# Attention and experts in float32: in each first product one of seven inner products moved to the end, onto a sum that ScalarE puts into PSUM

## The chip, the cores and the metric

The kernel runs on one core of a Trainium2 chip. The metric is the device time of one execution in microseconds (us); the time before is the median of three runs. One further execution was taken by the profiler, and all readings of instructions come from that one. TensorE is called PE in the profile, VectorE DVE, ScalarE ACT, GpSimd POOL, and SyncE, which issues most transfers, SP.

## The reference

All arrays are float32. A block-wise linear attention with decay is followed by four dense experts whose outputs are added with weights.

```
# attention: B,H,S,D = 4,8,768,64; blocks of 64 positions
intra = (qb @ kb.T) * Dmask            # Dmask[i,j] = lam^(i-j) for i >= j
out_b = intra @ vb + (qb * lam^(i+1)) @ state
state = lam^64 * state + (kb * lam^(63-i)).T @ vb
x = out -> (B*S, H*D) = (3072, 512)

# experts: N,D,E,F = 3072,512,4,1024
p = domain_probs / (domain_probs.sum(-1) + 1e-9)
out = sum over e of p[:, e] * (relu(x @ w1[e]) @ w2[e])
```

## The kernel before

**Tiles.** The 3072 tokens are three groups of 1024. A *unit* is one group with one expert, twelve in all (`units`). For a unit the *first product* is relu(x @ w1), the *second product* is that times w2. TensorE works on the second product of one unit and the first product of the next unit in turn.

**The recursion.** Each first product is done with seven products instead of eight (Strassen's scheme in Winograd's form), and each of these seven again with seven. The outer seven are run in the order `SEQ`: M1, M5, M6, M2, M7, M3, M4. Each outer product is what the texts call a *group*: seven inner products, one step of `inner(i)` each, in the order `INNER`. An inner product is two matmuls (two records each in the trace) of 128x128 weights by 128x256 tokens. It writes a PSUM bank of 128x512 (`pg`). The scheme adds inner products up: M1, M6, M5 and M3 all add into the bank `g1`, and M7 and M4 into the bank `g3`; M2 takes `g3` anew. After each inner product the bank is read out (`READ`), since the partial sum is itself a summand of one of the four blocks ("quarters") of the result: after M1 block 11, after M7 block 22, after M6 block 21, after M4 it is added to 21, after M5 to 22, after M2 to 11, after M3 block 12. ScalarE copies (L1055) where nothing older is to be added, otherwise VectorE adds (L117, through the helper `tt`).

Three of the outer products, M2, M3 and M4 (`OUT`), finish a quarter of the unit's result. ScalarE then applies Relu in SBUF (L1059). In units 5 to 11 (`NEST` is 5), whose second product is also done with two levels of seven, GpSimd then multiplies the quarter by the tokens' gates (`gated`, queued in `aside`).

**The order of TensorE's work.** It is written out by hand in *slots*, eight to each outer product. With a are the steps of the first product, with b those of the second, each list being handed out two by two or one by one:

```
order = [b[0:2], a[0:2], b[2:4], a[2:4], b[4:6], a[4:6], b[6:8], a[6:8]]    # both nested
order = [b[0:1], a[0:2], b[1:2], a[2:4], b[2:3], a[4:6], b[3:5], a[6:8]]    # second product not nested
```

So a[4:6], the fifth and the sixth inner product, stand directly one after the other, and a piece of the second product stands before and after the pair. Between slots, planned work of VectorE and GpSimd is taken from the lists `background`, `lately`, `own_sums` and `aside`, and a planner (`pump`) starts transfers and weight sums by estimated times of the engines. The engines then execute their own instructions in the order in which they were written.

**Attention** of the second and third group runs in the same slots: `turn` (transposes), `scores` (L694, L701) four slots later, `values` ten slots later. The attention's tokens that come through DRAM (`comes_across`) have other distances. The first group's attention and the first product of the first unit (`direct_product`, tiles `pM` and `pc`, L1502) run ahead of all slots.

**Gates.** `gates` computes p on VectorE during the direct product and then lays it out with 32 small VectorE copies (L571, L573): 16 into `gate`, 16 into `last_gate`.

Of the kernel before, what the change touches and what calls it, by code (L numbers as in the profile page):

```python
# [11 lines left out]
AF = mybir.ActivationFunctionType  # L12
ALU = mybir.AluOpType
# [8 lines left out]
def kernel(  # L22
# [30 lines left out]
    nc = tc.nc  # L53

    B, H, S, D = q.shape
    E, DM, F = moe_w1.shape
    NTOK, DOUT = out.shape
    P = nc.NUM_PARTITIONS
# [3 lines left out]
    NCH = S // C  # L62
    CPG = 8
    G = CPG * C
    NG = NTOK // G
    Q = G // 4
    DH = DOUT // 2
    W = 512
# [20 lines left out]
    def bank(tag, name):  # L89
        return ps.tile([P, W], FP32, name=name, tag=tag)  # L90
# [25 lines left out]
    def tt(eng, o, a, b, op):  # L116
        eng.tensor_tensor(out=o, in0=a, in1=b, op=op)  # L117
        if eng is nc.gpsimd:
            busy[0] = max(busy[0], now[0]) + math.prod(o.shape[1:]) / (640 if spare else 480)
        else:  # L120
            vector(math.prod(o.shape[1:]), PSUM in (a.space, b.space))

    def vector(n, psum):
        filled[0] = max(filled[0], now[0] + psum / 2) + 0.09 + n * (0.31 if psum else 0.8 if spare else 0.49) / 512
# [11 lines left out]
    LAST = NG - 1  # L136
    ORDER = {0: (0, 1, 2, 3), 1: (1, 2, 3, 0), LAST: (2, 3, 0, 1)}
    units = [(g, e) for g in range(NG) for e in ORDER[g]]
    unit_of = {u: x for x, u in enumerate(units)}
    NEST = 2 * E - 3  # L140
    FINAL = len(units) - 1

    def token(g, half, x):
        c, b = (half, x) if g == 0 else (2 * g + x % 2, 2 * (x // 2) + half)
        return b * S + c * C

    def where_of(n):
        return n // CPG, n % CPG // 4, n % 4
# [173 lines left out]
    INNER = ("M1", "M7", "M6", "M4", "M5", "M2", "M3")  # L322
# [145 lines left out]
    def comes_across(n):  # L468
        return where(n)[0] >= SECOND
# [47 lines left out]
    for r in range(2):  # L517
        for ac in range(NHP):
            h = 4 * r + ac
# [31 lines left out]
    gates_of = decay[:, 7, 0:96].rearrange("p (t e) -> p t e", e=E)  # L551
# [7 lines left out]
    def gates():  # L559
        total = decay[:, 6, 96:120]  # L560
        nc.vector.reduce_sum(out=total, in_=probs, axis=AX.X)
        nc.vector.tensor_scalar_add(out=total, in0=total, scalar1=1e-9)
        nc.vector.reciprocal(out=total, in_=total)
        nc.vector.tensor_tensor(
            out=gates_of, in0=probs, in1=total.unsqueeze(2).to_broadcast([P, NTOK // P, E]), op=ALU.mult,
        )

        for n in range(NG * CPG):
            t = token(*where_of(n)) // P
            if n < LAST * CPG:  # L570
                nc.vector.tensor_copy(out=gate[:, n], in_=gates_of[:, t])  # L571
            if n >= CPG:
                nc.vector.tensor_copy(out=last_gate[:, (n - CPG) * E:(n - CPG + 1) * E], in_=gates_of[:, t])  # L573

    def turn_gates():
        p, o = bank("s0", "gp"), small("gr")
# [101 lines left out]
    def scores(n, tags):  # L678
        all_added()
        while n not in turned:  # L680
            take(lately, True)
        qT, kT = turned[n][0:2]
        while any(f in lately for f in turned[n][3:]):
            take(lately, True)
        begin_state(n)
        kd, vn = nat.pop((n, "kd")), nat[n, "v"]
        first, last = where(n)[0] == 0, where(n)[0] == NCH - 1

        sp = [bank(tags[r], "sp") for r in range(2)]
        blk = [slice(x * BL, (x + 1) * BL) for x in range(2)]  # L690
        for ac in range(NHP):
            for r in range(2):
                for x in range(2):
                    nc.tensor.matmul(  # L694
                        out=sp[r][half[x], ac * BL:(ac + 1) * BL], lhsT=hc(kT)[half[r], ac, blk[x]],
                        rhs=hc(qT)[half[r], ac, blk[x]], start=(ac == 0), stop=True, skip_group_check=True,
                    )
        for ac in range(NHP):
            for x in range(1 if last else 2):
                for r in range(2):  # L700
                    nc.tensor.matmul(  # L701
                        out=sp[x][half[r], 256 + ac * D:256 + (ac + 1) * D], lhsT=kd[half[x], 2 * ac + r],
                        rhs=vn[half[x], 4 * r + ac], start=False, stop=True, skip_group_check=True,
                    )
        st = small("st")
        added = [sp[x][:, 256:512].rearrange("p (h d) -> p h d", d=D) for x in range(2)]

        def mask(r):
            tt(
                nc.vector, st[:, r * 256:(r + 1) * 256], sp[r][:, 0:256], s_decay[:, r].rearrange("p h c -> p (h c)"),  # L710
                ALU.mult,
            )

        def middle():
            s = states[n][:, 1]
            if first:
                nc.scalar.copy(out=s, in_=added[0])
            else:
                tt(nc.vector, s, s, added[0], ALU.add)

        def end():
            s = states[after_of(n)] = small("kv")[:].rearrange("p (x h d) -> p x h d", x=2, d=D)
            passed(nc.vector, s[:, 0], states[n][:, 1])
            tt(nc.vector, s[:, 0], s[:, 0], added[1], ALU.add)

        work = [lambda: (mask(0), mask(1)), middle] + ([] if last else [end])
        soon(n, *work)
        masked[n] = st, work
# [86 lines left out]
    def attention(g):  # L815

        def put(slot, f):
            steps.append((slot, f))

        for i in range(CPG):  # L820
            n, s = g * CPG + i, BEGIN[g][0] + BEGIN[g][1] * i
            put(s - 10, lambda n=n: load_more(n))
            put(s - 6, lambda n=n: load(n, "v"))
            put(s, lambda n=n: turn(n, ("s0", "s1")))
            if comes_across(n):
                put(s - 2, lambda n=n: (decayed(n), nat.pop((n, "k"))))
            put(s + (6 if comes_across(n) else 4), lambda n=n: scores(n, ("s0", "s1")))
            put(s + (12 if comes_across(n) else 10), lambda n=n: values(n, ("s0", "s1")))
            if n == NG * CPG - 1:
                put(s + 17, turn_gates)  # L830
        steps.sort(key=lambda s: s[0])
# [40 lines left out]
    outer = {e: {n: {} for n in ("B11", "B12", "B21", "B22", "T1", "T2", "T3", "T4")} for e in range(NEST, len(units))}  # L872
    within = {}

    def gated(e, i, j, at, t):

        def step():
            n = j * 4 + (int(at[1]) - 1) * 2
            x = t[:].rearrange("p (c t) -> p c t", c=2)
            by = gate_bc[:, n:n + 2].rearrange("p n t -> p (n t)").unsqueeze(1).to_broadcast([P, 2, 256])  # L880
            tt(nc.gpsimd, x, x, by, ALU.mult)
            outer[e][f"B{i + 1}{j + 1}"][at] = t

        aside.append(after(2, step))
# [133 lines left out]
    def settle(m, blocks):  # L1018

        while m in ("M7", "M4") and blocks["left"]:  # L1020
            rest(force=True)

    def first_product(g, e, m, blocks, tags):

        while (g, e, m) not in fed:
            pump(force=True)
        while unit_of[g, e] in (1, 2 * E) and to_do.get(m):
            take(own_sums, True)
        until(("x", g, m))
        ws, t = fed.pop((g, e, m)), slots[m]  # L1030
        xs = {i: t[:, X_AT[i]] for i in X_AT}
        settle(m, blocks)
        old = {
            "M1": None, "M5": None, "M6": blocks.get("M1"), "M2": blocks.get("M1"), "M7": blocks.get("U2"),
            "M3": blocks.get("U4"), "M4": blocks.get("U3"),
        }[m]
        new = {n: small("m" + n) for n in ("11", "12", "21", "22")} if m in ("M1", "M5", "M6") else old
        banks = {}

        def inner(i):  # L1040
            t = tags[0] if i in ("M1", "M6", "M5", "M3") else tags[1]
            fresh = i in ("M1", "M7", "M2")
            if fresh:
                banks[t] = bank(t, "p" + t)
            p = banks[t]
            for j in range(2):
                nc.tensor.matmul(  # L1047
                    out=p[:, j * 256:(j + 1) * 256], lhsT=ws[i][:, j * P:(j + 1) * P], rhs=xs[i],
                    start=(fresh and j == 0), stop=True, skip_group_check=True,
                )  # L1050
            at, begins = READ[i]
            if not begins:
                tt(nc.vector, new[at][:], p[:], new[at][:], ALU.add)
            elif old is None:
                nc.scalar.copy(out=new[at][:], in_=p[:])  # L1055
            else:
                tt(nc.vector, new[at][:], p[:], old[at][:], ALU.add)
            if m in OUT and (at == "12" or not begins):
                nc.scalar.activation(out=new[at][:], in_=new[at][:], func=AF.Relu)  # L1059
                if unit_of[g, e] >= NEST:  # L1060
                    gated(unit_of[g, e], *OUT[m], at, new[at])

        return [lambda i=i: inner(i) for i in INNER] + [lambda: finished(g, e, m, blocks, new)]


    acc = {}
# [721 lines left out]
```

## Time and profile before

| What | Value |
|---|---|
| Median of three runs | 1160.16 us (1159.94 to 1162.94) |
| Profiled execution | 1160.99 us |
| Its span | 1159.2 us |
| TensorE: first products (`pg` with streamed weights) | 1960 records, 382 ns mean as modelled |
| Mean of a VectorE addition from PSUM, 128x512 (`m<-pg,m`) | 688 ns |
| ScalarE copy PSUM to SBUF, 128x512 (`m<-pg`) | 586 ns |
| ScalarE copy SBUF to PSUM, 128x512 (`hp<-m`) | 590 ns |
| ScalarE Relu in SBUF, 128x512 | 630 ns |
| GpSimd multiplication by gates, 128x512 | 1289 ns |
| Gate copies on VectorE (L571 and L573) | 16 and 16, 5.5 and 2.3 us |

A row of a group gives the line, the engine, the operation, what it writes and reads, the shapes and the count; behind the first bar the busy time and the mean of one in ns; behind the second the engine's idle time just before these instructions, and what ended it. "PEld" is the loading of weights into TensorE. The duration of a matmul record is modelled and longer than the distance at which records follow each other. A row of the timeline gives start and duration in us; instructions of one kind that follow each other are merged (x8). Transfers issued by SyncE stand among the timeline's rows and are left out where none is spoken of.

### The profile page before, as it was taken

The page shows a single profiled execution, that of the slowest core. Times are in us where ns is not written, and L with a number is a line of the kernel's source. Part 1 is how long each engine was busy: PE and PEld are TensorE (multiplying, and loading weights), DVE is VectorE, ACT ScalarE, POOL GpSimd, SP SyncE. Part 2 cuts the span into 40 slices and gives each one's busy share as a digit, 9 for nine tenths or more (in the row PEclk, how much of TensorE's full clock was granted, in tenths as well). Part 3 has the DMA queues.
Part 4 walks back from the last instruction along what each step waited for, and adds up shares of the span by engine and source line. Part 5 has one row for each costly group of instructions (what it writes and reads, how often), then busy time and mean ns, then how long its engine had stood idle before and what let it go on. Part 6 is the DMA issues. An engine that isn't in the chain of part 4 may idle for free.

```text
span 1159.2 us, 22045 instructions
## 1 busy us (share of the span) xinstructions
PE 1143.5 (99%) x8011; PEld 991.6 (86%) x8011; DVE 836.6 (72%) x1516; ACT 317.0 (27%) x638; POOL 796.3 (69%) x752
## 2 busy tenths in 40 slices
PE   8999999999999999999999999999999999999998
PEld 7778888888888888888888888888888888888887
DVE  4597885578478857946775667999876667777785
ACT  4312122112201211221243341332343341341232
POOL 2747417646742985764795898996896883793894
PEclk9999999999999999999999999999999999999999
DMA  8795677999899999896867659976678757566552
GB/s 191 178 289 164 177 196 214 288 283 296 265 313 310 277 309 305 267 337 207 272 207 241 185 161 311 297 244 207 207 233 271 218 181 215 171 189 193 159 191 73
DMA packets 309259, 269.21 MB, mean 232 GB/s; under 512 B 141536, under 2 KB 244128, under 8 KB 309152
## 3 DMA queue, kind: packets, MB, share of 16 engines
q1 hardware_dynamic: 290832, 262.53, 74.2%
q10 hardware_dynamic: 18320, 5.28, 2.1%
q8 instruction: 64, 1.05, 0.4%
q14 instruction: 43, 0.35, 0.1%
HBM read 194.83 MB, written 77.10 MB: 235 GB/s over the span
## 4 chain that ended last, share of the span: by engine, by line
PE 88%; DVE 7%; DMA 2%; POOL 1%; issue 1%; SPq 0%; ACT 0%; ACTq 0%; DVEq 0%; POOLq 0%
PE pg L1047 38%; PE pq L1400 22%; PE q L1101 19%; DVE m L117 3%; PE pM L1502 2%; DVE sums L117 1%; PE sp L694 1%; PE op L748 1%; DVE xs L117 1%; PE op L766 1%; PE sp L701 1%; DMA kn<-in_k_dram 1%; PE kp L664 1%; PE pc L1502 1%; PE qp L664 1%
## 5 line engine op out<-in xcount | busy, mean ns | idle before, releaser
L1047 PE MATMUL pg<-xs,ws_in 128*128 128x256 f32 x1960 | 473.2, 382 | 2.5 <-DVE m L117 2.3
L1047 PEld LDWEIGHTS pg<-xs,ws_in 128*128 128x128 f32 x1960 | 369.0, 190 | 57.2 <-DVE m L117 7.9
L117 DVE TENSOR_TENSOR m<-pg,m 128x512 f32<-128x512 f32 x451 | 307.5, 688 | 121.0 <-PE pg L1047 107.5
L1101 PE MATMUL q<-w2t,m 128*128 128x256 f32 x1120 | 265.0, 380 | 0.0
L1101 PEld LDWEIGHTS q<-w2t,m 128*128 128x128 f32 x1120 | 213.0, 190 | 29.0 <-DVE m L117 0.5
L117 POOL TENSOR_TENSOR m<-m,decay 128x512 f32<-128x512 f32 x112 | 141.9, 1289 | 80.9 <-ACT m L1059 73.0
L1400 PE MATMUL pq<-acc,w2t 128*128 128x256 f32 x688 | 169.6, 380 | 0.2 <-DVE sums L117 0.2
L117 DVE TENSOR_TENSOR sums<-pq,sums 128x256 f32<-128x256 f32 x272 | 112.9, 420 | 67.4 <-PE pq L1400 58.5
L1400 PEld LDWEIGHTS pq<-acc,w2t 128*128 128x128 f32 x688 | 130.6, 190 | 18.6 <-issue 0.5
L1059 ACT ACTIVATE m<-m 128x512 f32<-128x512 f32 x132 | 82.9, 630 | 197.6 <-DVE m L117 190.9
L117 DVE TENSOR_TENSOR m<-m,m 128x512 f32<-128x512 f32 x112 | 100.5, 897 | 3.5 <-ACT m L1059 3.5
L1055 ACT COPY m<-pg 128x512 f32<-128x512 f32 x88 | 51.5, 586 | 146.7 <-PE pg L1047 143.5
L1119 DVE SCALAR_TENSOR_TENSOR acc<-q,gate,acc 128x256 f32<-128x256 f32 x108 | 51.9, 481 | 51.7 <-PE q L1101 51.4
L117 POOL TENSOR_TENSOR acc<-hT,hT 128x512 f32<-128x512 f32 x56 | 70.5, 1276 | 12.1 <-PE pq L1400 12.1
L117 POOL TENSOR_TENSOR acc<-hT,acc 128x512 f32<-128x512 f32 x56 | 71.4, 1275 | 6.5 <-PE pq L1400 2.6
L1400 PE MATMUL pq<-hT,w2t 128*128 128x256 f32 x288 | 74.1, 380 | 0.1
L979 ACT COPY up<-m 128x512 f32<-128x512 f32 x56 | 32.5, 588 | 126.8 <-DVE m L117 116.1
L117 POOL TENSOR_TENSOR w2o<-w2b 128x512 f32<-128x512 f32 x26 | 35.1, 1374 | 46.4 <-DMA w2b<-in_moe_w_dram 42.0
L1400 PEld LDWEIGHTS pq<-hT,w2t 128*128 128x128 f32 x288 | 54.7, 190 | 7.8 <-DVE sums L117 0.5
L899 ACT COPY hp<-m 128x512 f32<-128x512 f32 x84 | 48.4, 590 | 41.6 <-DVE hT L117 21.5
L1400 PE MATMUL pq<-m,w2t 128*128 128x256 f32 x228 | 58.5, 380 | 0.1
L117 POOL TENSOR_TENSOR xs<-xs 128x256 f32<-128x256 f32 x28 | 24.4, 873 | 43.1 <-DMA xs<-x_blocks 41.4
(140 smaller groups left out, 1368.3 us busy)
## 6 DMA issues: line engine op xcount, KB each, us to landing
w2t<-w_ops SPq DMA_DIRECT2D x129, 256.0 KB, 3.0
ws_in<-w_ops SPq DMA_DIRECT2D x40, 512.0 KB, 5.1
ws_in<-w_ops SPq DMA_DIRECT2D x60, 256.0 KB, 3.9
ws_in<-w_ops SPq DMA_DIRECT2D x40, 384.0 KB, 4.3
w2b<-in_moe_w_dram SPq DMA_DIRECT2D x56, 256.0 KB, 5.3
w_ops<-ops SPq DMA_DIRECT2D x28, 512.0 KB, 4.7
w2t<-w_sums SPq DMA_DIRECT2D x40, 256.0 KB, 4.7
w_sums<-w2o SPq DMA_DIRECT2D x16, 512.0 KB, 5.0
```

What stands on the lines that cost most here:

```text
L117: eng.tensor_tensor(out=o, in0=a, in1=b, op=op)
L664: nc.tensor.transpose(out=x[:, ac * C:(ac + 1) * C], in_=y[:, 2 * ac:2 * ac + 2].rearrange("p r d -> p (r d)"), identity=ident[:],)
L694: nc.tensor.matmul(out=sp[r][half[x], ac * BL:(ac + 1) * BL], lhsT=hc(kT)[half[r], ac, blk[x]], rhs=hc(qT)[half[r], ac, blk[x]], start=(ac ...
L899: nc.scalar.copy(out=there[x][:], in_=blk[at][:])
L979: nc.scalar.copy(out=there[at][:], in_=a[at][:])
L1047: nc.tensor.matmul(out=p[:, j * 256:(j + 1) * 256], lhsT=ws[i][:, j * P:(j + 1) * P], rhs=xs[i], start=(fresh and j == 0), stop=True, skip ...
L1055: nc.scalar.copy(out=new[at][:], in_=p[:])
L1059: nc.scalar.activation(out=new[at][:], in_=new[at][:], func=AF.Relu)
L1101: nc.tensor.matmul(out=p[:, s * DH:(s + 1) * DH], lhsT=h[A_OF[m]][:, c * 256 + s * P:c * 256 + (s + 1) * P], rhs=fed2[g, e, m][uu][:, c], ...
L1119: nc.vector.scalar_tensor_tensor(out=o, in0=x, scalar=w, in1=o, op0=ALU.mult, op1=ALU.add)
L1400: nc.tensor.matmul(out=p[:, 0:256], lhsT=fed3[e, m, x // 2][:, x % 2, c * P:(c + 1) * P], rhs=b[B_OF[i]][:, c * 256:(c + 1) * 256], start= ...
L1502: nc.tensor.matmul(out=p[:, s * 256:(s + 1) * 256], lhsT=a[c][:, f:f + P], rhs=b[:, c, j * 256:(j + 1) * 256], start=(s == 0 and c == 0 an ...
```

## The change

Four things are altered.

- The inner products run in the order `FIRST`: M3 is now the sixth and M2 the last.
- M2 no longer takes the bank `g3` anew and no longer is added to block 11 by VectorE. Just ahead of M3's matmuls, ScalarE copies block 11, as M1 left it, into `g3` (`seed`), and M2's matmuls add onto that copy. The sum is then read out once (`last`): by a ScalarE copy in outer products that are not final, by a ScalarE Relu in final ones of units before `NEST`, and in final ones of the later units by one VectorE operation that takes the maximum with zero and multiplies by the gates, so that neither Relu nor GpSimd's multiplication is made for that quarter.
- The gates are laid out by seven ScalarE copies.
- `scores` comes five slots after `turn`, where it was four, for tokens that do not come through DRAM.

```diff
-        for n in range(NG * CPG):
-            t = token(*where_of(n)) // P
-            if n < LAST * CPG:
-                nc.vector.tensor_copy(out=gate[:, n], in_=gates_of[:, t])
-            if n >= CPG:
-                nc.vector.tensor_copy(out=last_gate[:, (n - CPG) * E:(n - CPG + 1) * E], in_=gates_of[:, t])
+        of = gates_of.rearrange("p (b c) e -> p b c e", c=NCH)
+        last = last_gate.rearrange("p (n e) -> p n e", e=E)
+        nc.scalar.copy(
+            out=gate[:, 0:CPG].rearrange("p (h x) e -> p h x e", h=2), in_=of[:, :, 0:2].rearrange("p b c e -> p c b e"),
+        )
+        for g in range(1, NG):
+            for h in range(2):
+                n = g * CPG + h * 4
+                for to in ([gate[:, n:n + 4]] if g < LAST else []) + [last[:, n - CPG:n - CPG + 4]]:
+                    nc.scalar.copy(
+                        out=to.rearrange("p (b c) e -> p b c e", c=2), in_=of[:, h::2, 2 * g:2 * g + 2],
+                    )
...
-            put(s + (6 if comes_across(n) else 4), lambda n=n: scores(n, ("s0", "s1")))
+            put(s + (6 if comes_across(n) else 5), lambda n=n: scores(n, ("s0", "s1")))
...
+    FIRST = ("M1", "M7", "M6", "M4", "M5", "M3", "M2")
...
+        def seed():
+            banks[tags[1]] = bank(tags[1], "p" + tags[1])
+            nc.scalar.copy(out=banks[tags[1]][:], in_=new["11"][:])
+
+        def last(p, o):
+            if m not in OUT:
+                nc.scalar.copy(out=o[:], in_=p[:])
+            elif unit_of[g, e] < NEST:
+                nc.scalar.activation(out=o[:], in_=p[:], func=AF.Relu)
+            else:
+                i, j = OUT[m]
+                vector(W, True)
+                nc.vector.scalar_tensor_tensor(
+                    out=o[:].rearrange("p (c t) -> p c t", c=2), in0=p[:].rearrange("p (c t) -> p c t", c=2), scalar=0.0,
+                    in1=by_gate(j, "11"), op0=ALU.max, op1=ALU.mult,
+                )
+                outer[unit_of[g, e]][f"B{i + 1}{j + 1}"]["11"] = o
+
         def inner(i):
             t = tags[0] if i in ("M1", "M6", "M5", "M3") else tags[1]
-            fresh = i in ("M1", "M7", "M2")
+            fresh = i in ("M1", "M7")
             if fresh:
                 banks[t] = bank(t, "p" + t)
+            if i == "M3":
+                seed()
             p = banks[t]
...
             at, begins = READ[i]
+            if i == "M2":
+                last(p, new["11"])
+                return
...
-        return [lambda i=i: inner(i) for i in INNER] + [lambda: finished(g, e, m, blocks, new)]
+        return [lambda i=i: inner(i) for i in FIRST] + [lambda: finished(g, e, m, blocks, new)]
```

`by_gate` is the view of the gates that `gated` already used, taken out into a function of its own.

More of the change, by code (lines that the diff above doesn't have):

```diff
@@ L873, with by_gate @@
     within = {}
+    def by_gate(j, at):
+        n = j * 4 + (int(at[1]) - 1) * 2
+        return gate_bc[:, n:n + 2].rearrange("p n t -> p (n t)").unsqueeze(1).to_broadcast([P, 2, 256])
     def gated(e, i, j, at, t):
         def step():
-            n = j * 4 + (int(at[1]) - 1) * 2
             x = t[:].rearrange("p (c t) -> p c t", c=2)
-            by = gate_bc[:, n:n + 2].rearrange("p n t -> p (n t)").unsqueeze(1).to_broadcast([P, 2, 256])
-            tt(nc.gpsimd, x, x, by, ALU.mult)
+            tt(nc.gpsimd, x, x, by_gate(j, at), ALU.mult)
             outer[e][f"B{i + 1}{j + 1}"][at] = t
```

## The prediction

> **What bounds it now.** First the page's engine table and its costliest groups, then the waits of TensorE, then the timeline of two places.
>
> ```profile
> PE 1143.5 (99%) x8011; PEld 991.6 (86%) x8011; DVE 836.6 (72%) x1516; ACT 317.0 (27%) x638; POOL 796.3 (69%) x752
> ...
> L1047 PE MATMUL pg<-xs,ws_in 128*128 128x256 f32 x1960 | 473.2, 382 | 2.5 <-DVE m L117 2.3
> ...
> L117 DVE TENSOR_TENSOR m<-pg,m 128x512 f32<-128x512 f32 x451 | 307.5, 688 | 121.0 <-PE pg L1047 107.5
> ...
> L117 POOL TENSOR_TENSOR m<-m,decay 128x512 f32<-128x512 f32 x112 | 141.9, 1289 | 80.9 <-ACT m L1059 73.0
> ...
> L1059 ACT ACTIVATE m<-m 128x512 f32<-128x512 f32 x132 | 82.9, 630 | 197.6 <-DVE m L117 190.9
> ...
> L1055 ACT COPY m<-pg 128x512 f32<-128x512 f32 x88 | 51.5, 586 | 146.7 <-PE pg L1047 143.5
> ```
>
> TensorE is the bound: 99%, and VectorE and ScalarE mostly wait for it (107.5 and 143.5 us). Whatever relieves the others is worth only what TensorE waits for them. Its waits:
>
> ```profile
> PE pM L1502 <- DVE m L117: 2.5, 1, 2.5
> PE pg L1047 <- DVE m L117: 2.3, 7, 0.8
> ...
> PE sp L701 <- POOL kn L117: 1.3, 1, 1.3
> ```
>
> These are the prizes. The view counts from the modelled end of a matmul, so I took the starts in the timeline instead: matmul records of 128x256 follow each other every 216 ns (two records to a matmul, so an inner product of a first product is four, 0.86 us). Nine times a `pg` record starts 0.2 to 0.9 us late on a VectorE read, 3.9 us together. The largest:
>
> ```profile
> 730.40 0.68 DVE L117 TENSOR_TENSOR m<-pg,m 128x512 f32<-128x512 f32 x1
> ...
> 731.13 1.59 PEld L1047 LDWEIGHTS pg<-xs,ws_in 128*128 128x128 f32 x8 [1.17 <-DVE m L117]
> 731.13 1.99 PE L1047 MATMUL pg<-xs,ws_in 128*128 128x256 f32 x8 [0.77 <-DVE m L117]
> ...
> 732.97 1.89 PE L1400 MATMUL pq<-acc,w2t 128*128 128x256 f32 x8
> ```
>
> The read ends at 731.08 and the matmul starts 0.054 us later; the eight records then take 1.84 us instead of 8 x 0.216 = 1.73, because the first interval is 0.320. All nine show both figures: a wait costs the lateness of the read, plus 0.054, plus 0.104 us of restart.
>
> Last, one undisturbed group (M2 of the unit before last), from its M5 on:
>
> ```profile
> 983.69 1.89 PE L1047 MATMUL pg<-xs,ws_in 128*128 128x256 f32 x8
> 984.75 0.69 DVE L117 TENSOR_TENSOR m<-pg,m 128x512 f32<-128x512 f32 x1 [0.44 <-PE pg L1047]
> 985.42 1.03 PE L1400 MATMUL pq<-hT,w2t 128*128 128x256 f32 x4
> 985.48 0.63 ACT L1059 ACTIVATE m<-m 128x512 f32<-128x512 f32 x1 [1.96 <-DVE m L117]
> 985.62 0.69 DVE L117 TENSOR_TENSOR m<-pg,m 128x512 f32<-128x512 f32 x1 [0.17 <-PE pg L1047]
> 986.28 1.03 PE L1047 MATMUL pg<-xs,ws_in 128*128 128x256 f32 x4
> ```
>
> The eight records are inner M5 (bank g1) and inner M2 (bank g3). M5 has streamed at 984.55; VectorE reads g1 from 984.75 to 985.44. Only then may the next product add into g1. That is M3, at 986.28: M2 and a piece of the second product lay between, 1.73 us in all, and hid the read.
>
> **The change, part by part.**
>
> *The order M5, M3, M2.* M5 and M3 both add into g1, and M3 now directly follows M5 on TensorE; the build's listing shows M3 waiting for VectorE with nothing between. So the read of M5 (block 22, still an add on VectorE) is exposed in every group: 11 units x 7 products = 77 groups. In the 77 groups before, from the end of M5's streaming (last start + 0.216) to the end of its read took 0.89 us at least, under 1.00 in 55, 2.78 at most, 85.1 together; the excess over 0.89 is VectorE still busy with earlier items of its queue. In 73 groups the same instructions stand on VectorE between the reads of M4 and M5 as before; in four, one addition to a state (`kv`, 0.42 us) is now ahead of the read, and in one of these an addition of 0.7 has gone from there: +1. In eight groups M4's read was late already; the pauses will have drained some of that: I take off 4. So 82 us of lateness, and 77 x (0.054 + 0.104) = 12.2: **+94 us**. Bounds: all at the floor, 77 x 0.89 + 77 x 0.054 = 73; all backlog kept and a little more, 88 + 12 = 100. In the nine waits no later matmul overtook the waiting one; behind M3 stand the piece of the second product, M2 and all later groups, so nothing fills the pause. Nor can an earlier read help: M3's wait was for M5's read before as well (at 765.51 M3 started 0.05 us after it).
>
> In all nine waits the weight load began with its matmul, 2 ns or less ahead of it, as the two rows at 731.13 show. [...]
>
> What the pauses do to the clock: the 2.5 us wait at 78.9 left the granted clock (third figure from the end) of its stretch at 1.00, and the new pauses are shorter. I add nothing.
>
> ```profile
> 50.00:100.00 50.00, 47.54 (x279) 41.36 (x278) 40.81 (x85) 10.53 (x20) 27.92 (x23) 1.00 0.72 210
> ```
>
> [...]
>
> *The copy into PSUM and the quarter read out by ScalarE.* 77 seeds at 0.59 us (the `hp<-m` copies, SBUF to PSUM, take 590 ns), 44 copies out at 0.586, 12 Relus that merely read PSUM, 21 Relus of 0.63 gone: +45 +26 -13 = +58 us for ScalarE, idle 73% of the time. VectorE loses 77 additions of 0.688 (53 us) and gains 21 max-and-multiply operations: between 0.69 (the addition from PSUM) and 0.90 (the one from SBUF), 0.75 taken as it too reads one PSUM operand, 16 us. GpSimd loses 21 multiplications by gates of 1.289, 27 us. None of this is on the path but through the waits: the seed needs g3 free (M4's read, over 1.1 us before M5's end but in a few groups) and, in the three products with Relu, stands on ScalarE behind the Relu of M5's quarter; that starts 0.04 us after M5's read, so the seed ends about 1.23 us after it. M2 comes 0.16 (restart) + 0.86 (M3) + 0.86 (piece of the second product) = 1.88 us after the same read in the nested units, more in the others. Cover 0.6 us; nothing is added. Without that cover (one more ScalarE copy of 0.59 ahead of the seed) the 18 Relu groups of nested units would pay up to 0.5 us each, 10 us. What queues behind a waiting seed on ScalarE is M3's copy or Relu, which cannot begin before M3 ends. The read-out of M2 has a part of the second product and M1 before M7 needs g3: 2.6 us, against 0.2 + 0.6 to 0.9.
>
> *What is saved.* The nine waits go: M1 now comes one inner product later after M3's read, and the M3 waits are counted anew above: 3.9 + 9 x 0.104 = 4.9. The gates: 32 VectorE copies (5.5 + 2.3 us) between the reads of the direct product go to seven ScalarE copies of 0.24 to 0.6 us, beside idle time; behind them stood the reads that TensorE awaited at 78.9: 2.5 + 0.1, if the read comes in time, for a queue shorter by 6.6 us (68.58 to 75.19). The scores a slot (1.73 us) later: the keys that GpSimd finished at 185.97 are then there, 1.3 to 1.5 saved; no other scores waited. Together **-9 us**; between -5, if the order of GpSimd's chores moves, and -10.
>
> *Sum.* 94 - 9 = +85. Span 1159.2 + 85 = 1244; the profiled execution took 1160.99 (1.8 around the span), 0.83 above the median 1160.16. On the median: **1245 us**.
>
> **Rivals.** (a) The same wait, and the seed late too: for it, the seed queues behind waiting Relus; against, the 0.6 us of cover. +94 - 9 + 10 to 15: 1255 to 1260. (b) Faster: M3's wait is met early and costs nothing, so that the 9 us of savings remain: 1151. Its place is M3 alone; it decides when a pause costs under 9 / 77 = 0.12 us. For it: only the engine waited for is listed, not the instruction. Against: the bank holds M5's sum until it is read, and the read's floor is 0.89 us. (c) No pause at M3, but the seed becomes the wait: then M2 would stand 1.73 us after M5's end in the 18 nested Relu groups while the seed ends at 0.89 + 1.23 = 2.12: 18 x (0.39 + 0.16) = 10 us lost against 9 won, 1161.
>
> **Numbers.** Forecast 0.84, (a) 0.11, (b) 0.02, (c) 0.03. The bounds for faster and slower are 0.3% (3.5 us), about what a measurement of this kernel can tell from no change. Low end: lateness at its floor without the restart, 73 less 9, is +64; backlog not all vanishing, +70: 1230. High end: 100 - 5 and some of (a), +102: 1262. Faster 0.02, same 0.03, slower 0.95.
>
> **What would show it.** Right: `pg` waits on VectorE's `m` in TensorE's waits, about 77 times and some 70 to 90 us in starts, each at an M3 with the read ending 0.05 us before; VectorE near 790 us busy, ScalarE near 375, GpSimd near 770; clock 1.00; no `pM` and no `sp` wait. Wrong: few `pg` waits (b); waits on ScalarE's `pg` copy (a, c); a clock below 1.00.

## The result and the profile after

| What | Before | After |
|---|---|---|
| Median | 1161.49 us (1159.94 to 1162.94, 4 runs) | 1250.21 us (1247.29 to 1252.54, 4 runs) |
| Ratio, 95% interval | 1 | 1.0759 [1.074, 1.0777] |
| Profiled execution | 1160.99 us | 1250.49 us |
| Its span, mean granted clock | 1159.2 us, 1.000 | 1248.7 us, 0.996 |

The change costs 88.7 us on the medians and 89.5 us between the two profiled executions. The forecast was 1245 us, 5 us below the measurement.

First the engine table and the costliest groups of the page after, the lines that answer to those shown of before:

```profile
PE 1162.8 (93%) x8011; PEld 988.7 (79%) x8011; DVE 785.9 (63%) x1428; ACT 371.9 (30%) x745; POOL 768.0 (62%) x731
...
L1077 PE MATMUL pg<-xs,ws_in 128*128 128x256 f32 x1960 | 491.5, 385 | 67.6 <-DVE m L117 67.6
...
L117 DVE TENSOR_TENSOR m<-pg,m 128x512 f32<-128x512 f32 x374 | 256.2, 688 | 155.1 <-PE pg L1077 140.1
...
L1052 ACT COPY pg<-m 128x512 f32<-128x512 f32 x77 | 45.2, 588 | 140.4 <-DVE m L117 133.3
```

TensorE runs the same 8011 matmul records but is busy for 93% instead of 99%. The idle time ahead of the first product's matmuls went from 2.5 to 67.6 us, all of it ended by VectorE. VectorE itself works less than before (785.9 against 836.6 us) and waits longer for TensorE (140.1 against 107.5): both engines wait for each other in turn. The waits of TensorE in the same trace:

```profile
PE pg L1077 <- DVE m L117: 74.7, 76, 2.5
```

Seventy-six waits on one releaser stand where there were seven, all of them of M3 (the 77th M3 is listed under GpSimd, 0.9 us); the lines for `pM` and for `sp` on GpSimd, 2.5 and 1.3 us before, are gone. The last view is the timeline of after at the group that the prediction showed (M2 of the unit before last), from its inner M5 on:

```profile
1061.52 1.03 PE L1077 MATMUL pg<-xs,ws_in 128*128 128x256 f32 x4
...
1062.58 0.69 DVE L117 TENSOR_TENSOR m<-pg,m 128x512 f32<-128x512 f32 x1 [0.44 <-PE pg L1077]
1063.31 0.63 ACT L1092 ACTIVATE m<-m 128x512 f32<-128x512 f32 x1 [1.96 <-DVE m L117]
1063.32 0.73 PEld L1077 LDWEIGHTS pg<-xs,ws_in 128*128 128x128 f32 x4 [1.19 <-DVE m L117]
1063.33 1.13 PE L1077 MATMUL pg<-xs,ws_in 128*128 128x256 f32 x4 [0.78 <-DVE m L117]
1063.84 0.58 ACT L1052 COPY pg<-m 128x512 f32<-128x512 f32 x1
...
1065.16 1.03 PE L1077 MATMUL pg<-xs,ws_in 128*128 128x256 f32 x4
```

M5 has streamed at 1062.38. VectorE reads `g1` from 1062.58 to 1063.27, and M3 starts at 1063.33: 0.95 us without a matmul, where before M2 stood. The seed (L1052) runs behind the Relu and ends at 1064.42, 0.74 us ahead of M2 at 1065.16, which starts on time.

### The profile page after: what moved, and what is told of

It is laid out like the page before. It is cut to its first block, busy times and chain, and to the rows that moved or that the text cites. A ratio compares the mean times of both kernels' runs of the same rounds, so it can differ in the third digit from the quotient of the medians.

```text
span 1248.7 us, 22113 instructions
## 1 busy us (share of the span) xinstructions
PE 1162.8 (93%) x8011; PEld 988.7 (79%) x8011; DVE 785.9 (63%) x1428; ACT 371.9 (30%) x745; POOL 768.0 (62%) x731
## 3 DMA queue, kind: packets, MB, share of 16 engines
q8 instruction: 64, 1.05, 0.4%
## 5 line engine op out<-in xcount | busy, mean ns | idle before, releaser
L1077 PE MATMUL pg<-xs,ws_in 128*128 128x256 f32 x1960 | 491.5, 385 | 67.6 <-DVE m L117 67.6
L117 DVE TENSOR_TENSOR m<-pg,m 128x512 f32<-128x512 f32 x374 | 256.2, 688 | 155.1 <-PE pg L1077 140.1
L117 POOL TENSOR_TENSOR m<-m,decay 128x512 f32<-128x512 f32 x91 | 114.9, 1274 | 121.7 <-ACT m L1092 98.1
L1092 ACT ACTIVATE m<-m 128x512 f32<-128x512 f32 x99 | 62.4, 630 | 182.2 <-DVE m L117 175.2
L117 DVE TENSOR_TENSOR m<-m,m 128x512 f32<-128x512 f32 x112 | 95.6, 855 | 11.0 <-ACT m L1056 5.6
L1088 ACT COPY m<-pg 128x512 f32<-128x512 f32 x88 | 51.6, 586 | 140.6 <-PE pg L1077 137.5
L1052 ACT COPY pg<-m 128x512 f32<-128x512 f32 x77 | 45.2, 588 | 140.4 <-DVE m L117 133.3
L1056 ACT COPY m<-pg 128x512 f32<-128x512 f32 x44 | 25.8, 586 | 124.4 <-PE pg L1077 120.0
```

The lines of the kernel that those rows point to most:

```text
L1052: nc.scalar.copy(out=banks[tags[1]][:], in_=new["11"][:])
L1056: nc.scalar.copy(out=o[:], in_=p[:])
L1077: nc.tensor.matmul(out=p[:, j * 256:(j + 1) * 256], lhsT=ws[i][:, j * P:(j + 1) * P], rhs=xs[i], start=(fresh and j == 0), stop=True, skip ...
```

## The experiments

All ratios are to runs of the kernel before on the same chip, with 95% intervals. "Late" means, as in the prediction, how far a record's start in the timeline lies behind the end of streaming of the one before it on TensorE, which for a record of 128x256 is 0.216 us after that one's start. For orders of slots, a is the first product's list of steps and b the second's, as in the kernel.

### The order by itself, in the kernel before

No seed; gates and scores as before. VectorE still adds M2's sum to block 11.

```diff
-        return [lambda i=i: inner(i) for i in INNER] + [...]
+        first = ("M1", "M7", "M6", "M4", "M5", "M3", "M2")
+        return [lambda i=i: inner(i) for i in first] + [...]
```

> The kernel before with the order alone changed to M1, M7, M6, M4, M5, M3, M2; M2 still takes g3 anew and VectorE still adds it to block 11, gates and scores as before. Theory: the whole loss comes from this, 77 waits at M3 of 0.95 us and more, 96 us with their restarts, less the waits of M1 and M3 of before (5 us): 1250 to 1260, a few us above the changed kernel, which has the savings of gates and scores. Rival (the copies that ScalarE puts into PSUM carry part of the loss): clearly below the changed kernel, 1200 to 1240.

Measured: 1252.76 us, ratio 1.0779 [1.0752, 1.0806]. The waits of TensorE in this run:

```profile
PE pg L1047 <- DVE m L117: 72.4, 77, 2.1
...
PE pM L1503 <- DVE m L117: 2.5, 1, 2.5
```

All 77 inner M3 start late, 84.9 us together and 8.1 us of restart. This one edit loses as much as the whole change, and M3's pauses are about as large without the seed (84.9 us) as with it (88.1): the loss is the order M5, M3. The `pM` wait stays, since the gates were not touched.

### M2 between M5 and M3

The changed kernel with the old order of the last two products; so that the seed is ready, it is issued ahead of M5.

```diff
-    FIRST = ("M1", "M7", "M6", "M4", "M5", "M3", "M2")
+    FIRST = ("M1", "M7", "M6", "M4", "M5", "M2", "M3")
...
-            if i == "M3":
+            if i == "M5":
                 seed()
```

> The changed kernel with M2 put back between M5 and M3 (order M1, M7, M6, M4, M5, M2, M3), and block 11 copied into g3 just ahead of M5 instead of M3; all else as changed. Theory (the exposed read of M5 costs some 96 us, and the clock falls after the longest pauses another 3 to 5): the pauses at M3 go from 88 us in starts to under 3, and the time is 1149 to 1155, below the kernel before. Rival (the seed is what costs): M2 now has to wait for a copy that has less time, at least 0.5 us in the 18 groups with Relu beside a nested second product and more elsewhere, and the time stays above 1163.

Measured: 1173.17 us, ratio 1.0097 [1.0083, 1.0111]. M3's lateness falls from 88 to under 2 us, so the pauses were M3's. But a new wait has come, on the seed:

```profile
PE pg L1077 <- ACT pg L1052: 9.5, 21, 1.9
```

M2 follows M5 directly, and the seed needs M4's read of `g3` and its own 0.59 us first. In starts it is 23 waits, 13.3 us and 2.4 us of restart, 14 of them in units whose second product isn't nested, where fewer pieces lie between M4 and M5. Both readings were right in part: M3's pause is cured, and a rival's wait on the seed takes its place.

### The gates alone, the scores alone

Each is that part of the change put into the kernel before, and nothing else: the seven ScalarE copies in place of the 32 on VectorE, and

```diff
-            put(s + (6 if comes_across(n) else 4), lambda n=n: scores(n, ("s0", "s1")))
+            put(s + (6 if comes_across(n) else 5), lambda n=n: scores(n, ("s0", "s1")))
```

> The kernel before with the gates laid out by seven ScalarE copies, nothing else. Theory: the 2.5 us wait of TensorE at 78.9 us (pM on VectorE) goes, with 0.1 us of restart, and all later work moves up by it: 1158 to 1159.5. Rival: the next VectorE operation of the direct product is late anyhow, under 0.5 us gained, 1160.5 to 1162.

> The kernel before with the scores a slot later, nothing else. Theory: the 1.3 to 1.5 us wait of TensorE for the decayed keys (sp on GpSimd at 185.9 us) goes and no new wait comes: 1159 to 1160.5. Rival: the later state additions stand ahead of reads of the first product on VectorE, and TensorE waits for those instead, 1161 or above.

The gates alone: 1158.91 us, ratio 0.9979 [0.997, 0.9989]. The waits of TensorE begin with

```profile
PE op L772 <- issue: 2.4, 1, 2.4
PE pg L1053 <- DVE m L117: 2.3, 6, 0.8
```

and have no line for `pM`. The step is worth 2.4 us of the ratio, 2.7 of the profiled times, as it was worked out.

The scores alone: 1161.14 us, ratio 1.0000 [0.9988, 1.0011]. The wait at 186.0 is gone: GpSimd's keys are done at 186.59 and the scores start at 187.05. Yet TensorE now waits 1.2 us ahead of a transpose at 247.2, where before there was no wait, and 1.2 instead of 0.6 us for an M1 at 389.7. What was saved is given back later.

### A piece of the second product between M5 and M3

M2 stays last; a piece of the second product that stood ahead of M5 now stands between M5 and M3.

```diff
-order = [b[0:2], a[0:2], b[2:4], a[2:4], b[4:6], a[4:6], b[6:8], a[6:8]]
+order = [b[0:2], a[0:2], b[2:4], a[2:4], b[4:5], a[4:5] + b[5:6] + a[5:6], b[6:8], a[6:8]]
...
-order = [b[0:1], a[0:2], b[1:2], a[2:4], b[2:3], a[4:6], b[3:5], a[6:8]]
+order = [b[0:1], a[0:2], b[1:2], a[2:4], [], a[4:5] + b[2:3] + a[5:6], b[3:5], a[6:8]]
```

> The changed kernel with one piece of the second product moved between M5 and M3: 0.86 us beside a nested second product (M4, piece, M5, piece, M3), 1.73 us otherwise (M4 and M5 now adjacent, then the piece, M3). Theory (a pause is the lateness of the read less what stands between, plus 0.05 and 0.10 of restart): about 0.08 + 0.10 us is left in each of 77 groups, at M3 in the nested ones and at M5, which waits for M6's read, in the others, 14 us, plus what VectorE's longer queues still show, 5 to 12: 1165 to 1178. Rival (the seed on ScalarE is a second wait of its own, as it was with M2 between M5 and M3): M2 waits 0.5 us and more in the 33 groups with Relu, and the time is 1182 or more.

Measured: 1211.4 us, ratio 1.0426 [1.0403, 1.0449]. More than half of the loss stays, far more than expected. TensorE's waits in this run:

```profile
PE pg L1077 <- DVE m L117: 33.9, 50, 1.8
PE qp L670 <- issue: 6.6, 4, 2.0
```

In 11 of the 42 nested groups M3 starts 0.946 to 0.948 us after M5's end, just what the read takes, and the piece covers nearly all of it. In the others it is 1.13 to 2.80. The piece was taken from the place ahead of M5, so M5 comes one piece sooner behind the same work on VectorE, and VectorE's queue is late instead: in the 11 groups VectorE was idle just before the read, in each of the other 31 it went into the read straight from earlier work. In starts 43 M3 are late by 34.7 us together, and 14 M5, which waited for nothing much before, by 9.0. A cover moved from ahead of the awaited product to behind it gives, here, only part of its length. Of M2's seed no wait was seen. The four `qp` waits of 6.6 us in all stay open: the profile names no releaser for them.

### M3 a whole slot later, beside M2

M5 stands alone in its slot, and M3 and M2 share the last one. One or more pieces of the second product then lie between M5 and M3 (1.73 us in the group whose timeline follows), and M5 has as many ahead of it as in the changed kernel.

```diff
-order = [b[0:2], a[0:2], b[2:4], a[2:4], b[4:6], a[4:6], b[6:8], a[6:8]]
+order = [b[0:1], a[0:2], b[1:3], a[2:4], b[3:5], a[4:5], b[5:8], a[5:8]]
...
-order = [b[0:1], a[0:2], b[1:2], a[2:4], b[2:3], a[4:6], b[3:5], a[6:8]]
+order = [b[0:1], a[0:2], b[1:2], a[2:4], b[2:3], a[4:5], b[3:5], a[5:8]]
```

Run with the rest of the change as it is, and with the scores four slots after `turn` again:

> The changed kernel with the slots handed out so that 1.73 us of the second product stand between M5 and M3, and M3 and M2 follow each other in the last slot. Theory: both the read of M5 (0.89 us) and the seed behind M5's Relu (2.17 us after M5's end, M2 being 2.59 after it) have their cover, the 96 us and the lows of the clock go and gates keep their 2.6: 1149 to 1156, below the kernel before. Rival (the seed or ScalarE's longer queue still holds TensorE, as in the order with M2 between): M2 waits 15 us and more in total and the time is 1163 or more.

> The run before this one with the scores four slots after turn again. Theory (the scores' slot bought nothing by itself): within 2 us of it either way. Rival (with the new slots the later scores keep their 1.5 us): 1 to 2 us slower.

Measured: 1170.79 us, ratio 1.0082 [1.0064, 1.01]; with the scores at four 1174.52 us, 1.0109 [1.0092, 1.0125]. M3's lateness falls to under 2 us. What is late next is the seed, as the rival had it. TensorE's waits and one group of the timeline, both of the run with the scores at five:

```profile
PE pg L1077 <- ACT pg L1052: 5.3, 11, 0.9
PE pq L1433 <- DVE sums L117: 3.2, 3, 2.3
```

```profile
1111.08 0.63 ACT L1092 ACTIVATE m<-m 128x512 f32<-128x512 f32 x1 [1.03 <-DVE m L117]
...
1111.61 1.10 ACT L907 COPY hp<-m 128x512 f32<-128x512 f32 x2
...
1112.64 0.58 ACT L1052 COPY pg<-m 128x512 f32<-128x512 f32 x1
...
1113.28 0.73 PEld L1077 LDWEIGHTS pg<-xs,ws_in 128*128 128x128 f32 x4 [0.84 <-ACT pg L1052]
```

ScalarE does a Relu and two `hp` copies first; the seed is done at 1113.22, and M2 starts 0.06 later. In starts M2 waits for the seed 23 times, 10.1 us and 2.4 of restart. Issued just ahead of M3, the seed stands behind everything that ScalarE was given up to then. That the scores' place is worth 3.7 us here and nothing alone was not expected. In the trace with the scores at four, one M2 at 190.1 waits 2.5 us for its seed, and the wait for `sums` near the end is 0.8 us longer; why they come with the scores' place was not followed up.

### The same order without the seed, and with the seed issued earlier

The first is the kernel before with the gates by ScalarE, the new order of products and the slots above; VectorE adds M2's sum. The second is the changed kernel with those slots and the seed ahead of M5:

```diff
-            if i == "M3":
+            if i == "M5":
                 seed()
```

> The kernel before with ScalarE's gates and with the order and slots of the second run of this call, but M2 still takes g3 anew and VectorE still adds it to block 11; scores at four slots. It prices the quarter that is added up in PSUM. Theory (VectorE's 53 us of additions are worth only the waits of M1 and M3 for VectorE, 5 us): 1153 to 1160, between 1 and 5 us slower than with the seed. Rival (VectorE is not late anywhere in this order, so the seed buys nothing): within 1 us of the run with the seed, or faster.

> The run with M3 and M2 in the last slot, with block 11 copied into g3 ahead of M5's matmuls instead of M3's, so that the copy stands on ScalarE ahead of M5's Relu and of the copies for the sums of later units. Theory (the seed was late because it stood in ScalarE's queue behind instructions that wait for VectorE): M2's 23 waits for the copy, 10 us with 2.4 us of restart, go, and the time is 1157 to 1161. Rival (the seed is late because block 11 itself or M4's read is late): the waits stay, 1168 or more.

Measured: without the seed 1165.13 us, ratio 1.0031 [1.0018, 1.0044]; with the seed ahead of M5 1160.68 us, ratio 0.999 [0.9976, 1.0003]. M2 waits for nothing in either. Both lose time at one place near the end: a `pq` wait on VectorE's `sums`, of 3.8 us at its longest in the first and of 3.2 in the second.

### The wait near the end

VectorE there stands at the transpose of result rows `y` (L1386), which come back through DRAM (`gather`). In the kernel before, these transposes waited for no transfer; that the new slots bring them closer to it is an inference, which the next runs bear on. Two ways out were tried on the kernel with the seed ahead of M5: the transpose a slot later, or the gather three slots sooner.

```diff
-                then(6 if n != order[0] else 14, (), lambda n=n: gather(n))
-                then(6, (), lambda n=n: turn_rows(n))
+                then(6 if n != order[0] else 14, (), lambda n=n: gather(n))
+                then(7, (), lambda n=n: turn_rows(n))
```

> The run before this one with the eight transposes of the parked result (VectorE, y) taken seven planned slots after their transfers instead of six. In the run with M3 and M2 in the last slot one of them waited for its transfer at 1122.75 us, VectorE's queue stood behind it, TensorE waited 2.3 us for a sum, and the clock fell for 3.4 us. Theory: both go, 1153 to 1157. Rival (the transfers have shifted by more than a slot): no gain, within 1 us of the run before this one.

Measured: 1160.55 us, ratio 0.9983 [0.9972, 0.9993]. The wait stayed: the transpose at 1110.25 waited 2.10 us for the transfer, and TensorE 2.7 us behind it. A later place in the list did not help.

```diff
-                then(6 if n != order[0] else 14, (), lambda n=n: gather(n))
+                then(3 if n != order[0] else 14, (), lambda n=n: gather(n))
```

> The run with the seed ahead of M5, with the transfers of the parked result (gather) asked for three planned slots after the step before them instead of six; the transposes keep their six. In the two runs before this one the last of the eight transposes fell behind the last first product, where slots are short, and stood 2.1 us waiting for its transfer, with TensorE behind it. Theory: the last transpose comes some 15 to 20 us earlier, beside the last first product; TensorE's wait of 2.7 to 3.2 us and the low of the clock of 1.7 go: 1155 to 1158. Rival (the transposes wait wherever they stand, or VectorE is then late for others): 1159 or more.

Measured: **1154.8 us, ratio 0.9954 [0.9939, 0.997]**, better than both kernels. The transposes in the groups by line, ahead of this edit and with it:

```profile
L1386 DVE STREAM_TRANSPOSE y<-y 128x512 f32<-128x512 f32 x8 | 5.6, 702 | 2.6 <-DMA y<-parked 2.6
```

```profile
L1386 DVE STREAM_TRANSPOSE y<-y 128x512 f32<-128x512 f32 x8 | 5.6, 701 | 0.0
```

The 2.6 us for the transfer are gone, and so is a stretch of half clock behind TensorE's wait there (ahead of this edit, six matmul records took 2.90 us from 1113.68 on; the mean granted clock was 0.998 there and is 0.999 with it). TensorE is back at 99%:

```profile
PE 1141.7 (99%) x8011; PEld 992.0 (86%) x8011; DVE 790.4 (69%) x1428; ACT 371.5 (32%) x745; POOL 772.8 (67%) x731
```

Last, whether the seed has a part in that gain: the same slots, gates, scores and gather, but no seed, VectorE adding M2's sum.

> The last run without the quarter added up in PSUM: M2 takes g3 anew and VectorE adds it to block 11; order, slots, gates, scores and the earlier gather as there. It prices the seed alone. Theory (the 53 us of additions taken from VectorE are worth only TensorE's waits for late reads, some 3 to 5 us in this order): 1157 to 1161, TensorE waiting more for VectorE at M3 and M6. Rival (with the reads covered by the order, VectorE's load no longer matters): within 1.5 us of the last run's 1154.8.

Measured: 1160.13 us, ratio 0.998 [0.9966, 0.9994]. Against the runs of the kernel before that go with each, this gains 2.6 us, with the seed it is 5.65. Late VectorE reads are back: four M3 with 2.2 us together, one of them 1.4, where with the seed there were two with 0.6; and one second product by 1.0 us, where there was none. So the seed is worth some 3 us, once its own place is covered, and these late reads fit that it gains by relieving VectorE; the two intervals overlap slightly, so the size is rough.

## Why the prediction was right

- **The order M5, M3.** Forecast 82 us of lateness and 12.2 of 0.054 and restart, 94; measured 88.1 in starts (which hold the 0.054) and 7.9 of restart (0.104 in 70 of the 77), 96. No M3 is less than 0.945 us late and 34 of the 77 lie at 0.945 to 0.948: the floor of 0.89 plus 0.054. That the backlog would mostly stay was right to 2 us. The swap alone, with 84.9 us in starts, showed that the rest of the change adds some 3 us to it at most.
- **The restart.** The rows at 1063.32 and 1063.33 show the weight load starting with its matmul, as in the nine waits before; in all 77 pauses the two starts lie 0.03 us apart or less. The first interval was 0.320 us in 70 of the 77 pauses (0.29 to 0.36 in the rest). The sum held: 7.9 us of restart, against the 77 x 0.104 = 8.0 of the forecast.
- **The seed's cover.** It held: no M2 waited for a seed, and none started less than 0.68 us behind its seed's end, against the 0.6 forecast. (The three terms behind the forecast's 1.23 us from M5's read to the seed's end, 0.04, 0.63 and 0.59, add up to 1.26; the group shown took 1.15, since the seed began before the Relu's end.) It was thin: where the place between seed and M2 got shorter or ScalarE had other work ahead (M2 between M5 and M3, and M3 beside M2), 23 of 77 seeds were late, 10 to 13 us in starts. Rival (a)'s mechanism is real, but not in this order.
- **The engines' loads.** VectorE 785.9 us, ScalarE 371.9, GpSimd 768.0, against some 790, 375 and 770. The max-and-multiply took 688 ns, like the addition from PSUM, where 0.75 was taken; the seven gate copies took 198 to 218 ns each, where 0.24 to 0.6 was taken.
- **The savings.** Forecast 9, found 11.4 by starts: 2.7 for the gates, 1.5 for the scores, and 7.2 for first products (7.0 us of late starts before, 2.2 after without the new pauses of M3, and 2.4 in the longer intervals behind late starts, of which the forecast counted 0.9). The gates' step was shown by itself. The scores' step was not right as put: alone it gains nothing, because its time comes back as other waits.
- **The clock: the step that failed.** "I add nothing" rested on one wait of 2.5 us that left the clock at 1.00. Three stretches of half clock appear in after, 3.413 us each, where before had none behind its first 7 us (1.00 from there to the end): two behind pauses of M3 (2.67 and 2.07 us late; a loss of 1.7 us each, 3.4) and one at 14.6 us into the span, in a gap of 2.40 us between two starts, which before had too (2.33), without the stretch. At 52 us after is 1.4 us behind before; that this is the third stretch's price is likely, but other small waits differ there too. The sum closes: 96.0 + 3.4 + 1.4 - 11.4 = 89.4, measured 89.5.

The error of 5 us is thus mostly the clock (4.8), with the 2 us more of M3's pauses and the 2.4 more of savings against each other. Rivals (b) and (c) needed M3's pause to cost nothing; it cost over 1.2 us in the mean.

## What to carry to other kernels

When two products add into one PSUM bank that must be read between them, count what stands between them on TensorE: here a read costs 0.95 us from the last matmul's end to the next one's start, 1.05 with the restart, and each group without cover pays it in full, however idle the reading engine is on average (VectorE was busy for 63% of the span). Moving work from VectorE to a quieter engine was worth some 3 us here, and the new order beat the kernel before only when the order of slots, the moved operation's place in its queue and a transfer that stood on the path in the new order were each put right. A wait that is removed alone may come back one stage later, as the scores' did, so test each part by itself and then the sum.

## What the hardware showed beyond that

In after, the granted clock fell to half in three stretches of 3.413 us. The windows view of after, with the granted clock third from the end: two stretches of 50 us with one such stretch each, then two windows of 3.41 us around the one behind M3's longest pause. It begins at 765.56, 0.24 us into the second window, whose mean is therefore 0.53.

```profile
750.00:800.00 50.00, 44.83 (x196) 38.25 (x197) 34.34 (x62) 9.70 (x17) 33.91 (x31) 0.97 0.87 270
900.00:950.00 50.00, 44.55 (x195) 37.64 (x195) 28.34 (x51) 22.77 (x46) 40.92 (x39) 0.97 0.70 223
```

```profile
761.91:765.32 3.41, 0.90 (x6) 0.45 (x4) 3.32 (x5) 0.59 (x1) 2.51 (x3) 1.00 0.86 264
765.32:768.73 3.41, 3.41 (x9) 2.73 (x10) 0.69 (x1) 0.00 (x0) 2.34 (x2) 0.53 0.92 259
```

In the second of these windows TensorE is busy throughout but gets through 9 records, since at half clock they follow each other every 0.427 us instead of 0.216.

The three stretches of after begin at 14.625, 765.557 and 929.397 us. The second follows the M3 that started 2.67 us late, at 765.28, the third one that started 2.07 late, at 928.87. The length of a pause alone does not tell which is followed by one: in the same trace M3 started 2.40 us late at 176.86, 2.09 at 326.83 and 2.08 at 944.82, and the windows of 6 us around these three have a granted clock of 1.00. So the wait of 2.5 us at 78.9 before, 2.62 by starts, also at 1.00, said nothing of what other pauses would do. What decides it, these runs do not show.
